# Attention output split into halves once, kept in DRAM for the MLP's second half; low halves of later weights on VectorE

## The chip, the cores and the metric

The kernel runs on one core of a Trainium2 chip. A core has TensorE (PE, matmuls, with its weight loads shown apart as PEld), VectorE (DVE), ScalarE (ACT), GpSimd (POOL) and SyncE (SP), which here only issues DMAs. Each engine takes its own instructions strictly in order and waits for others by semaphores. The metric is the device time of one execution in microseconds.

## The reference, cut to what matters

Attention with rotary embedding over 4 batches, 8 heads, 576 positions and head size 64; its output, reordered to x of 2304 tokens by 512, goes through two MLPs:

```python
x = np.ascontiguousarray(attn_out.transpose(0, 2, 1, 3)).reshape(B * S, H * D)
# first MLP: w_in 512 x 2048, w_out 2048 x 512
h = x @ w_in
g = h - np.tanh(h)
x = g @ w_out
# second MLP: w1, w2 512 x 1024, w3 1024 x 1024, w_out 1024 x 512
a = x @ w1
b = x @ w2
h = a * b @ w3
out = h @ w_out
```

The weights arrive as float64 and are read as pairs of 32-bit words.

## The kernel before, in words

**Halves.** A float32 factor is split into a high part, rounded to the type that TensorE takes (F32R), and a low part, the rest. A product is three matmuls: high by high, high by low, low by high. For weights the function `split` (L126) makes the high part on ScalarE (L127) and the low part on GpSimd (L128). For x the function `split_x` (L526) makes both on GpSimd (L528 and L529).

**Weights.** `load_raw` loads 512 KB of raw words on SP's queue into one of two buffers; `to_f32` makes float32 of them with two operations on ScalarE (L117, L119) and two on VectorE (L120, L122); `place` calls `split` into a slot. `next_conv` converts the next unit and issues the load of the one after the next. The order of the units is `half1` (`w_in` and `w_out`, first 1024 hidden units), the first part of w3 by the last `w_out` (`o2`, `w3`), `half2` (hidden units 1024 to 2047), the second part of that product, and `half3` (w1, w2). The slots of `half2` are those of `half1`, those of `half3` those of `half2`, so the conversions crowd at the turn from one to the next.

**Stages of the profiled execution.** Until about 323 us: attention. In it 16 pairs of heads run; VectorE takes row maxima (L329), ScalarE the exponentials (L336), GpSimd the normalization (L347), TensorE scores, transposes and products. From there to 809 us: the first MLP. Its tokens form five blocks: x0, x1, x2, the 256 tail tokens xt (block 4) and x3 (block 3), in this order, each with 8 steps of 128 hidden units, all of it twice, for the first and for the second half of the hidden units: `seq`, 80 steps, of which 0 to 39 are the first half. Step n is an h group (L546, 12 matmuls), `emit_g` (L559 to L569) and an x2 group (L583, 12 matmuls); h is emitted two steps ahead. `emit_g` computes h − tanh(h) on ScalarE (L559 to L562, L568) and VectorE (L563 to L566, L569) with a series for small h. The matrix w3 by the last `w_out` is folded in between (`wp_trans`, `wp_mm`) and goes to DRAM (`wp_dram`). From 809 us: the final stage, with w1, w2 and the folded matrix (`wpt`), whose input x2 is split by the same `split_x`.

**Splits of x.** The blocks are split once for each half, so twice: block p+1's first two of four parts in steps 5 and 6 of block p, the other two in step 7 (L714 to L721). The tiles `xs` share six buffers (X_BUFS) of 128 by 2 by 512; part 2 of the next block waits for a part of the current block to be free.

**Order.** The program's text gives a priority; a list scheduler of the framework places the instructions on each engine, and may hoist one out of a later stage where its inputs and buffers are ready. Conversions of `half1` that the text puts behind the attention stand within it on the engines for this reason.

## Time and profile before

| | |
|---|---|
| Median of 3 runs (lowest, highest) | 1117.77 us (1115.21, 1119.29) |
| Profiled execution, its own time | 1111.25 us |
| Its span, first to last instruction | 1109.4 us |
| TensorE busy | 1055.3 us, 95% |
| VectorE busy | 730.3 us, 66% |
| ScalarE busy | 598.9 us, 54% |
| GpSimd busy | 387.8 us, 35% |
| DMA queue q1 | 95.38 MB, 30.0% of 16 engines' span |

The shares are means over stages with different limits, so they tell little by themselves. A busy TensorE is not one at full speed: matmuls overlap, and their ends are modelled. The granted clock is 1.00 at 2.4 GHz; 0.86 in a stretch means that part of it ran at 1.2 GHz. DMA-issuing instructions and waits are not counted as busy.

### The profile page before, as it was taken

What the parts mean: (1) busy time and instruction counts of PE and PEld (TensorE: products, weight loads), DVE (VectorE), ACT (ScalarE), POOL (GpSimd) and SP (SyncE); (2) the same over time, 40 slices, a digit from 0 to 9 for tenths busy, and PEclk for the clock granted to TensorE, in tenths of its full rate; (3) what the DMA queues carried; (4) which work ended last, traced back from release to release, by engine and by line L of the source; (5) the groups of instructions that cost most, each with busy time, mean ns of one, the idle gap of its engine ahead of it and who ended that gap; (6) DMA issues with size and microseconds to landing.
All of it is one profiled execution on the core that took longest, in us unless ns stands there. A gap on an engine that the chain in (4) does not pass through costs nothing.

```text
span 1109.4 us, 15634 instructions
## 1 busy us (share of the span) xinstructions
PE 1055.3 (95%) x5598; PEld 853.6 (77%) x5598; DVE 730.3 (66%) x1300; ACT 598.9 (54%) x1262; POOL 387.8 (35%) x379
## 2 busy tenths in 40 slices
PE   5999999999998999998989999999799999999998
PEld 3777776777766888887767788898588888888887
DVE  6899988999649867669998867678952212212121
ACT  4688777777767655557767655556652111111121
POOL 5576675665461302014463220323630202001000
PEclk9899999999998999999999999999999999999999
DMA  6667675766403011023223102232740100101010
GB/s 195 171 161 173 182 178 140 186 176 147 99 20 106 10 57 58 32 64 95 77 76 113 38 10 76 87 105 86 246 133 1 38 1 1 38 1 38 1 38 20
DMA packets 64684, 96.36 MB, mean 87 GB/s; under 512 B 11616, under 2 KB 40288, under 8 KB 64608
## 3 DMA queue, kind: packets, MB, share of 16 engines
q1 hardware_dynamic: 64608, 95.38, 30.0%
q8 instruction: 44, 0.72, 0.3%
q14 instruction: 32, 0.26, 0.1%
HBM read 58.79 MB, written 11.01 MB: 63 GB/s over the span
## 4 chain that ended last, share of the span: by engine, by line
PE 68%; DVE 14%; ACT 7%; POOL 4%; DMA 4%; issue 2%; SPq 0%; DVEq 0%; ACTq 0%; POOLq 0%
PE pw L750 18%; PE x2p L583 11%; PE h L546 10%; PE o L773 9%; PE sc L325 6%; PE pv L410 4%; PE wp L630 3%; PE te L383 3%; DVE nm L329 2%; DMA raw_w<-in_moe_w 2%; DVE g_q L564 2%; ACT e L336 1%; DVE g_q L566 1%; PE pv L407 1%; DVE g_s L563 1%
## 5 line engine op out<-in xcount | busy, mean ns | idle before, releaser
L583 PE MATMUL x2p<-g,s_out 128*128 128x512 f32 (+1 forms) x960 | 223.4, 380 | 22.3 <-ACT g L568 12.8
L583 PEld LDWEIGHTS x2p<-g,s_out 128*128 128x128 f32 x960 | 172.2, 194 | 62.8 <-ACT g L568 18.3
L347 POOL TENSOR_SCALAR e<-e,r 128x576 f32<-128x576 f32 x144 | 121.8, 859 | 80.9 <-DVE r L345 35.8
L756 DVE TENSOR_TENSOR ab<-a,pw 128x512 f32<-128x512 f32 (+1 forms) x40 | 25.4, 635 | 182.9 <-PE pw L750 180.5
L336 ACT ACTIVATE e<-sc,nm 128x576 f32<-128x576 f32 x144 | 108.0, 750 | 47.2 <-DVE nm L329 31.5
L329 DVE TENSOR_REDUCE nm<-sc 128x1 f32<-128x576 f32 x144 | 106.8, 749 | 17.3 <-PE sc L325 16.5
L773 PE MATMUL o<-wpt,abs 128*128 128x512 f32 x432 | 104.5, 389 | 0.0
L325 PE MATMUL sc<-ks,qs 128*128 128x288 f32 x480 | 92.1, 321 | 3.2 <-ACT e L336 2.8
L563 DVE TENSOR_TENSOR g_s<-g_s,h 128x512 f32<-128x512 f32 (+1 forms) x80 | 50.5, 632 | 65.8 <-ACT g_m L562 65.6
L773 PEld LDWEIGHTS o<-wpt,abs 128*128 128x128 f32 x432 | 80.6, 188 | 16.4
L325 PEld LDWEIGHTS sc<-ks,qs 128*128 128x128 f32 x480 | 68.8, 190 | 26.7 <-ACT e L336 10.6
L383 PE MATMUL te<-ident,e 128*128 128x128 f32 x576 | 84.4, 278 | 5.1 <-POOL e L347 4.5
L754 ACT COPY a<-pw 128x512 f32<-128x512 f32 (+1 forms) x40 | 21.8, 544 | 117.9 <-PE pw L750 117.9
L568 ACT CAST g<-g_q 128x512 fp32r<-128x512 f32 (+1 forms) x80 | 46.1, 576 | 59.0 <-DVE g_q L566 58.6
L383 PEld LDWEIGHTS te<-ident,e 128*128 128x128 f32 x576 | 68.0, 142 | 11.7 <-POOL e L347 8.4
L559 ACT ACTIVATE g_s<-h 128x512 f32<-128x512 f32 (+1 forms) x80 | 44.1, 551 | 53.9 <-PE h L546 52.4
L569 DVE TENSOR_TENSOR g<-g_q,g 128x512 fp32r<-128x512 f32 (+1 forms) x80 | 58.1, 726 | 22.6 <-ACT g L568 21.7
L566 DVE COPY_PREDICATED g_q<-g_m,g_t 128x512 f32<-128x512 int32 (+1 forms) x80 | 69.1, 864 | 1.6
L758 ACT CAST abs<-ab 128x512 fp32r<-128x512 f32 (+1 forms) x40 | 23.0, 576 | 84.8 <-DVE ab L756 84.8
L564 DVE SCALAR_TENSOR_TENSOR g_q<-g_q,g_s 128x512 f32<-128x512 f32 (+1 forms) x80 | 62.6, 782 | 0.0
L560 ACT ACTIVATE g_q<-g_s,qb 128x512 f32<-128x512 f32 (+1 forms) x80 | 54.5, 682 | 0.2 <-DVE g L569 0.2
L562 ACT ACTIVATE g_m<-g_s,nt 128x512 f32<-128x512 f32 (+1 forms) x80 | 54.0, 676 | 0.0
(380 smaller groups left out, 2256.7 us busy)
## 6 DMA issues: line engine op xcount, KB each, us to landing
ks<-kp SPq DMA_DIRECT2D x60, 288.0 KB, 5.0
raw_w<-in_moe_w SPq DMA_DIRECT2D x32, 512.0 KB, 3.7
raw_in<-in_moe_w_in SPq DMA_DIRECT2D x16, 512.0 KB, 4.0
raw_out<-in_moe_w_out SPq DMA_DIRECT2D x16, 512.0 KB, 4.4
qs<-qp SPq DMA_DIRECT2D x60, 128.0 KB, 3.5
wp_dram<-wpe SPq DMA_DIRECT2D x24, 256.0 KB, 2.0
k<-in_k SPq DMA_DIRECT2D x16, 256.0 KB, 3.2
q<-in_q SPq DMA_DIRECT2D x16, 256.0 KB, 3.0
```

Of the source, the lines that this page charges most:

```text
L325: nc.tensor.matmul(s[:, n, 0:HS], lhs, rhs, start=t == 0, stop=t == len(terms) - 1)
L329: nc.vector.tensor_reduce(nm[:, j:j + 1], s[:, :, 0:HS], AX.XY, ALU.max, negate=True)
L336: nc.scalar.activation(d["e"][:, j, :].rearrange("p (n s) -> p n s", n=2), d["ss"][j][:, :, 0:HS], AF.Exp, bias=d["nm"][:, j:j + 1], accum ...
L347: nc.gpsimd.tensor_scalar(d["e"][:, j, :], d["e"][:, j, :], r[:, j:j + 1], 1.0, ALU.mult, ALU.mult)
L383: nc.tensor.transpose(ps[:, n * 128:(n + 1) * 128], e[:, o + n * 128:o + (n + 1) * 128], ident)
L546: nc.tensor.matmul(ps[:, 0:w], ws[:, a, kk], x[:, b_, 0:w], start=kc == 0 and t == 0, stop=kc == NK - 1 and t == 2)
L563: nc.vector.tensor_tensor(s, s, h, ALU.mult)
L564: nc.vector.scalar_tensor_tensor(qq, qq, QC, s, ALU.add, ALU.mult)
L566: nc.vector.copy_predicated(qq, mk.bitcast(I32), t)
L583: nc.tensor.matmul(x2ps[j][o][:, 0:w], ws[:, a, oo], g[:, b_, 0:w], start=c == 0 and t == 0, stop=c == HF - 1 and t == 2)
L750: nc.tensor.matmul(ps[:, 0:w], ws[:, a, kk], x[:, b_, 0:w], start=kc == 0 and t == 0, stop=kc == NK - 1 and t == 2)
L773: nc.tensor.matmul(outps[j][t], g[:, a, tt], wp[c][:, b_, :], start=c == 0 and i == 0, stop=c == NF2 - 1 and i == 2)
```

## The change

The tiles that `split_x` makes in the first half are written to DRAM (`xs_dram`, one tensor for each block) on SP's queue. In the second half `load_x` reads them back, in step 1 of the block before, instead of splitting again. Parts 2 and 3 of the blocks at places 0, 2 and 4 of the order go to the area of x3, which is then free, the others to `xs` buffers. From the end of the attention's text on, `split` makes the low part on VectorE: `lows[0]` is changed there. Counted over the program, 47 low parts (L128 before, L133 after) go from GpSimd to VectorE, and GpSimd loses the 20 splits (40 instructions) of the second half.

```diff
--- before.py
+++ after.py
@@ -78,6 +78,9 @@
     const.tile([128, 8], F32, name="half_line")
 
     wp_dram = dram.tile([DF2, 2, DM], F32, name="wp_dram")
+
+    xs_dram = [dram.tile([DM, 2, SM if j < B else B * ST], F32, name=f"xs_dram{j}")
+               for j in range(B + 1)]
 
     def slot(i, u):
         return slots.tile([128, 2, 512], F32R, tag=f"s{i}", name=f"s_{u[0]}{u[1]}")
@@ -123,9 +126,11 @@
             z, hi, -0x80000000, z, ALU.bitwise_and, ALU.bitwise_or)
         return z.bitcast(F32)
 
+    lows = [nc.gpsimd]
+
     def split(z, s):
         nc.scalar.copy(s[:, 0, :], z)
-        nc.gpsimd.tensor_tensor(s[:, 1, :], z, f32(s[:, 0, :]), ALU.subtract)
+        lows[0].tensor_tensor(s[:, 1, :], z, f32(s[:, 0, :]), ALU.subtract)
 
 
     pairs = [(b, hp) for b in range(B) for hp in range(NP)]
@@ -510,6 +515,7 @@
             pv(b, hp, c // 2)
     att.release()
     psum.release()
+    lows[0] = nc.vector
 
 
     ph2 = tc.alloc_tile_pool(name="ph2", bufs=2, side="right", reuse_waits="tile")
@@ -523,12 +529,26 @@
 
     xs = {}
 
-    def split_x(key, src, kc, w):
+    def split_x(key, src, kc, w, keep=None):
         t = ph2.tile([128, 2, SM], F32R, tag="xs", name=f"xs_{key}_{kc}", bufs=X_BUFS)
         nc.gpsimd.tensor_scalar(t[:, 0, 0:w], src[:, kc, :], 1.0, 1.0, ALU.mult, ALU.mult)
         nc.gpsimd.tensor_tensor(t[:, 1, 0:w], src[:, kc, :], f32(t[:, 0, 0:w]), ALU.subtract)
+        if keep is not None:
+            nc.sync.dma_start(keep[kc * 128:(kc + 1) * 128], f32(t[:, :, 0:w]))
         xs[key, kc] = t
 
+    def load_x(key, j, kc, w):
+
+        if order.index(j) % 2 == 0 and kc >= 2:
+            if kc == 2:
+                pair_x[0] = xpool.tile([128, 2, 2, SM], F32R, tag="x3", name=f"xl_{j}")
+            t = pair_x[0][:, kc - 2]
+        else:
+            t = ph2.tile([128, 2, SM], F32R, tag="xs", name=f"xl_{j}_{kc}", bufs=X_BUFS)
+        nc.sync.dma_start(f32(t[:, :, 0:w]), xs_dram[j][kc * 128:(kc + 1) * 128])
+        xs[key, kc] = t
+
+    pair_x = [None]
 
     order = [*range(B - 1), B, B - 1]
     seq = [(hf, j, c) for hf in range(2) for j in order for c in range(HF)]
@@ -646,7 +666,7 @@
 
     NS = len(seq)
     for kc in range(NK):
-        split_x((0, 0), x_t[0], kc, widths[0])
+        split_x((0, 0), x_t[0], kc, widths[0], xs_dram[0])
     emit_h(0)
     emit_g(0)
     emit_h(1)
@@ -711,14 +731,15 @@
             emit_h(m)
             emit_g(m)
 
-            if c2 in (HF - 3, HF - 2):
-                if m + HF - c2 < NS:
-                    hf3, j3, _ = seq[m + HF - c2]
-                    split_x((hf3, j3), x_t[j3], c2 - (HF - 3), widths[j3])
-            if c2 == HF - 1 and m + 1 < NS:
-                hf3, j3, _ = seq[m + 1]
-                for kc in (2, 3):
-                    split_x((hf3, j3), x_t[j3], kc, widths[j3])
+            p2 = order.index(j2) + hf2 * nblk
+            if c2 in (HF - 3, HF - 2, HF - 1) and p2 + 1 < nblk:
+                j3 = order[p2 + 1]
+                for kc in ((2, 3) if c2 == HF - 1 else (c2 - (HF - 3),)):
+                    split_x((0, j3), x_t[j3], kc, widths[j3], xs_dram[j3])
+            if c2 == 1 and nblk <= p2 + 1 < 2 * nblk:
+                j3 = order[p2 + 1 - nblk]
+                for kc in range(NK):
+                    load_x((1, j3), j3, kc, widths[j3])
         emit_x2(n)
         do(n)
```

In the order of instructions the names carry the step or unit, and at their ends a running number; line numbers of the changed kernel are its own, up to 20 higher.

VectorE, `emit_g` of step 44 (first MLP, second half) and the conversions among it, before:

```order
L563 TENSOR_TENSOR g_s_44_6639<-g_s_44_6639,h_44_6626 128x512
L565 TENSOR_TENSOR g_t_44_6641<-h_44_6626,g_t_44_6641 128x512
L564 SCALAR_TENSOR_TENSOR g_q_44_6640<-g_q_44_6640,g_s_44_6639 128x512
L120 SCALAR_TENSOR_TENSOR z_o27_7227<-z_o27_7227,raw_o27_7124 128x512
L566 COPY_PREDICATED g_q_44_6640<-g_m_44_6642,g_t_44_6641 128x512
L122 SCALAR_TENSOR_TENSOR z_o27_7227<-raw_o27_7124,z_o27_7227 128x512
L120 SCALAR_TENSOR_TENSOR z_w31_7276<-z_w31_7276,raw_w31_7176 128x512
L569 TENSOR_TENSOR g_44_6651<-g_q_44_6640,g_44_6651 128x512
L122 SCALAR_TENSOR_TENSOR z_w31_7276<-raw_w31_7176,z_w31_7276 128x512
```

VectorE, the same step after; L133 is the low part of a weight, L123 and L125 are the conversion (L120 and L122 before), L583 to L589 are `emit_g`:

```order
L583 TENSOR_TENSOR g_s_44_6667<-g_s_44_6667,h_44_6654 128x512
L585 TENSOR_TENSOR g_t_44_6669<-h_44_6654,g_t_44_6669 128x512
L584 SCALAR_TENSOR_TENSOR g_q_44_6668<-g_q_44_6668,g_s_44_6667 128x512
L133 TENSOR_TENSOR s_out15_6831<-z_out15_6824,s_out15_6831 128x512
L586 COPY_PREDICATED g_q_44_6668<-g_m_44_6670,g_t_44_6669 128x512
L123 SCALAR_TENSOR_TENSOR z_o24_7089<-z_o24_7089,raw_o24_6819 128x512
L125 SCALAR_TENSOR_TENSOR z_o24_7089<-raw_o24_6819,z_o24_7089 128x512
L589 TENSOR_TENSOR g_44_6679<-g_q_44_6668,g_44_6679 128x512
```

One low part, that of `s_out15`, stands between the third and the fourth operation of the chain; a unit is converted in this step as before, an earlier one than before, and only one.

SP, the loads of raw weights around the turn to the second half, before:

```order
L100 DMA raw_out12_6517<-in_moe_w_out 128x512
L94 DMA raw_in13_6611<-in_moe_w_in 128x4x128
L100 DMA raw_out13_6621<-in_moe_w_out 128x512
L94 DMA raw_in14_6671<-in_moe_w_in 128x4x128
L100 DMA raw_out14_6681<-in_moe_w_out 128x512
L94 DMA raw_in15_6734<-in_moe_w_in 128x4x128
```

SP after, where `xl_1` are the four parts of block 1:

```order
L103 DMA raw_out12_6545<-in_moe_w_out 128x512
L97 DMA raw_in13_6639<-in_moe_w_in 128x4x128
L103 DMA raw_out13_6649<-in_moe_w_out 128x512
L548 DMA xl_1_0_6515<-xs_dram1_87 128x1024
L548 DMA xl_1_1_6517<-xs_dram1_87 128x1024
L548 DMA xl_1_2_6519<-xs_dram1_87 128x1024
L548 DMA xl_1_3_6521<-xs_dram1_87 128x1024
L97 DMA raw_in14_6699<-in_moe_w_in 128x4x128
L103 DMA raw_out14_6709<-in_moe_w_out 128x512
L97 DMA raw_in15_6759<-in_moe_w_in 128x4x128
```

The four reads of block 1 stand between the loads of `raw_out13` and `raw_in14`.

ScalarE at the end of the first MLP, steps 78 and 79, with the conversions of `w13` and `w23`, before:

```order
L117 ACTIVATE z_w13_8727<-raw_w13_8594 128x512
L119 ACTIVATE raw_w13_8594<-raw_w13_8594 128x512
L117 ACTIVATE z_w23_8737<-raw_w23_8604 128x512
L559 ACTIVATE g_s_79_8534<-h_79_8521 128x512
L568 CAST g_78_8506<-g_q_78_8495 128x512
L560 ACTIVATE g_q_79_8535<-g_s_79_8534,qb_80 128x512
L561 ACTIVATE g_t_79_8536<-h_79_8521 128x512
L562 ACTIVATE g_m_79_8537<-g_s_79_8534,nt2_82 128x512
L127 CAST s_w13_8734<-z_w13_8727 128x512
L119 ACTIVATE raw_w23_8604<-raw_w23_8604 128x512
```

ScalarE at the same place after (L120, L122 and L132 are L117, L119 and L127 before; L579 to L582 and L588 are `emit_g`):

```order
L582 ACTIVATE g_m_78_8499<-g_s_78_8496,nt2_82 128x512
L132 CAST s_w22_8608<-z_w22_8601 128x512
L122 ACTIVATE raw_w13_8596<-raw_w13_8596 128x512
L579 ACTIVATE g_s_79_8536<-h_79_8523 128x512
L581 ACTIVATE g_t_79_8538<-h_79_8523 128x512
L580 ACTIVATE g_q_79_8537<-g_s_79_8536,qb_80 128x512
L588 CAST g_78_8508<-g_q_78_8497 128x512
L582 ACTIVATE g_m_79_8539<-g_s_79_8536,nt2_82 128x512
L132 CAST s_w13_8736<-z_w13_8729 128x512
L120 ACTIVATE z_w23_8739<-raw_w23_8606 128x512
L122 ACTIVATE raw_w23_8606<-raw_w23_8606 128x512
L588 CAST g_79_8548<-g_q_79_8537 128x512
```

The first operation on `raw_w23` stood ahead of `g_s_79`; it now stands behind the operations of step 79 up to `g_m_79`.

## Rows read from the trace of the kernel before

**Rows 1.** Stages, all engines: window in us, its length; busy us (instructions) of each engine; clock; DMA.

```profile
165.00:275.00 110.00, 103.80 (x750) 79.83 (x747) 103.41 (x235) 85.29 (x218) 66.58 (x72) 1.00 0.64 162
323.00:350.00 27.00, 22.82 (x92) 18.03 (x89) 22.02 (x24) 17.97 (x32) 14.63 (x12) 0.87 0.16 59
505.00:522.00 17.00, 14.13 (x83) 11.99 (x82) 15.49 (x22) 11.28 (x26) 11.08 (x9) 1.00 0.35 115
522.00:638.00 116.00, 105.80 (x437) 81.77 (x436) 103.21 (x138) 81.76 (x146) 48.00 (x35) 0.99 0.23 73
785.00:809.00 24.00, 17.07 (x61) 13.05 (x60) 21.44 (x24) 13.54 (x25) 15.49 (x12) 0.86 0.65 230
```

**Rows 2.** Waits of TensorE, 480 to 940 us: total us, times, longest.

```profile
PE x2p L583 <- ACT g L568: 8.6, 6, 3.0
...
PE x2p L583 <- DVE g L569: 7.2, 10, 1.6
...
PE h L546 <- POOL xs_(1, 0)_3_6402 L529: 2.2, 1, 2.2
```

**Rows 3.** Chain of waits, 630 to 640 us: start us, length, instructions.

```profile
632.39 2.72 PE x2p L583 x12
635.11 2.72 PE h L546 x12
```

**Rows 4.** Timeline of TensorE, 522 to 523 us: start us, length, instruction.

```profile
522.52 0.50 PE L583 MATMUL x2p<-g,s_out 128*128 128x512 f32 x1
```

**Rows 5.** Groups by line, VectorE, 522 to 638 us: count, busy us, mean ns, idle before.

```profile
L566 DVE COPY_PREDICATED g_q<-g_m,g_t 128x512 f32<-128x512 int32 x19 | 20.7, 1090 | 0.3
...
L564 DVE SCALAR_TENSOR_TENSOR g_q<-g_q,g_s 128x512 f32<-128x512 f32 x19 | 17.2, 903 | 0.0
...
L569 DVE TENSOR_TENSOR g<-g_q,g 128x512 fp32r<-128x512 f32 x19 | 14.9, 783 | 4.5 <-ACT g L568 4.1
...
L563 DVE TENSOR_TENSOR g_s<-g_s,h 128x512 f32<-128x512 f32 x19 | 13.0, 683 | 6.5 <-ACT g_m L562 6.4
...
L120 DVE SCALAR_TENSOR_TENSOR z_out<-z_out,raw_out 128x512 int32<-128x512 int32 x5 | 5.0, 1008 | 0.2 <-ACT z_out L117 0.2
```

**Rows 6.** Timeline of VectorE, 641 to 645 and 782 to 783 us, GpSimd idle.

```profile
641.99 0.68 DVE L564 SCALAR_TENSOR_TENSOR g_q<-g_q,g_s 128x512 f32<-128x512 f32 x1
642.71 0.75 DVE L566 COPY_PREDICATED g_q<-g_m,g_t 128x512 f32<-128x512 int32 x1
644.45 0.69 DVE L569 TENSOR_TENSOR g<-g_q,g 128x512 fp32r<-128x512 f32 x1 [0.99 <-ACT g L568]
...
782.40 0.69 DVE L120 SCALAR_TENSOR_TENSOR z_w<-z_w,raw_w 128x512 int32<-128x512 int32 x1
```

**Rows 7.** Timeline of VectorE, 327 to 334 us; in brackets the idle time before.

```profile
327.42 4.75 DVE L120 SCALAR_TENSOR_TENSOR z_o<-z_o,raw_o 128x512 int32<-128x512 int32 x1 [3.42 <-ACT z_o L117]
...
333.80 0.67 DVE L563 TENSOR_TENSOR g_s<-g_s,h 128x512 f32<-128x512 f32 x1
```

**Rows 8.** Groups by line, GpSimd, 522 to 638 us: count, busy us, mean ns.

```profile
L128 POOL TENSOR_TENSOR s_in<-z_in,s_in 128x512 fp32r<-128x512 f32 x6 | 10.0, 1668 | 1.4 <-ACT s_in L127 1.4
L128 POOL TENSOR_TENSOR s_out<-z_out,s_out 128x512 fp32r<-128x512 f32 x6 | 8.2, 1375 | 23.0 <-ACT s_out L127 23.0
```

**Rows 9.** Timeline of ScalarE and TensorE, 794 to 805 us; in brackets the idle time before.

```profile
794.32 0.66 ACT L117 ACTIVATE z_w<-raw_w 128x512 f32<-128x512 f32 x1 [2.81 <-DMA raw_w<-in_moe_w]
...
794.89 0.58 ACT L559 ACTIVATE g_s<-h 128x512 f32<-128x512 f32 x1
...
796.03 0.50 PE L583 MATMUL x2p<-g,s_out 128*128 128x512 f32 x1 [3.02 <-ACT g L568]
...
804.66 0.79 PE L583 MATMUL x2p<-g,s_out 128*128 128x512 f32 x1 [2.69 <-ACT g L568]
```

**Rows 10.** DMA issues by tensor: count, KB each, median us to landing.

```profile
raw_in<-in_moe_w_in SPq DMA_DIRECT2D x16, 512.0 KB, 4.0
...
wpt<-wp_dram SPq DMA_DIRECT2D x8, 512.0 KB, 7.1
```

## The prediction

> **What bounds the kernel now.** I read the windows by stage first. What can be gained in the MLP lies where TensorE is not busy throughout: its start (323 to 350), the turn from the first half of the hidden units to the second (505 to 638) and the last 24 us before the final stage (785 to 809, clock 0.86) [rows 1]. In the attention (165 to 275) TensorE and VectorE are both busy 94% of the time, so there either one may set the pace. Next, the waits of TensorE from 480 to 940 us: it waits for ScalarE's `g` (L568), VectorE's `g` (L569) and once for a split on GpSimd, L529 [rows 2]. Each is an end of the chain h, `emit_g`, x2. Third, the pace: at full speed an h group and an x2 group of 12 matmuls take 2.72 us each, so a step of the MLP takes 5.44 us. From the x2 group of step 32 of `seq`, which starts at 522.52, to that of step 49 at 632.39 lie 17 steps in 109.87 us; at full speed they need 92.5, and step 49 itself runs at full speed. So 17.4 us are lost in steps 32 to 49, which take 115.3 instead of 97.9 [rows 3, 4].
>
> The cause is VectorE. In 522 to 638 it is busy 103.2 of 116 us [rows 1], and its operations are stretched: COPY_PREDICATED (L566) takes 1090 ns on average, L564 903, L569 783, L120 of the conversion 1008 [rows 5], where the same operations take 750, 680, 690 and 690 with GpSimd idle [rows 6]. L563, which reads its second input from PSUM, is at 683 in the same window and is not stretched [rows 5]. So only operations whose inputs are all in SBUF suffer, and GpSimd is busy 48 of these 116 us [rows 1]. The worst is one L120 of 4.75 us at 327.42 [rows 7].
>
> The Trainium skill, "SBUF — State Buffer", section "SBUF: two separate sides", says that a VectorE operation with two SBUF inputs and a GpSimd operation that reads SBUF exclude each other for a whole instruction. The difference between L563 and the others agrees [rows 5]. By that rule alone one VectorE operation would lose at most one GpSimd instruction; the 4.75 us lost more than two of the 1.38 to 1.67 us splits [rows 7, 8], so I take the rows. The rule also speaks against the change, since the moved subtraction has two SBUF inputs; by it each of the five that fall into the attention may hold up L347 there by its own length, which lies inside the bound of +6 below.
>
> **The change part by part.** (a) 47 low halves (L128) go from GpSimd to VectorE: seven of the first half's weights, 8 `o2`, 16 and 16 of the later halves. On GpSimd one takes 1.38 to 1.67 us [rows 8]. VectorE's price is not in the trace; the nearest row is L569, the same subtraction with the same types: 0.69 us quiet, 0.78 mean in the crowded window [rows 5, 6]; the far end is a stretched L120, 1.01 [rows 5]. I take 0.69 where GpSimd has little left and 1.01 in the attention.
> (b) The 20 splits of x for the second half (L528, L529) disappear from GpSimd; 20 writes and 20 reads of DRAM appear on SP.
> (c) The scheduler reorders each engine.
>
> *Turn, steps 32 to 49.* What goes is the stretch: with the counts of the window, 19 × (1090−750) + 19 × (903−680) + 19 × (783−690) = 12.5 us for the g chain, and 5 × 0.32 = 1.6 for one group of L120: 14.1 [rows 5, 6]. Eleven more conversions have no row here; where they are stretched like this group they add up to 3, so some 17 in all. What comes is 20 splits × 0.69 = 13.8. From the order, VectorE's list for these 18 steps holds 18 × 5 operations of the chain (0.68+0.68+0.68+0.75+0.69 = 3.48: 62.6 us), 15 conversions of two operations (1.38: 20.7), 20 splits (13.8) and ten evictions from PSUM, three of half width, at or below L563's 0.68 (5.5): 102.6 us. TensorE needs 97.9, so VectorE is still the longer by 5. The chain also passes to ScalarE and back once a step; I allow 0.15 us a step for that, 2.7: 105.3 against 115.3, or −10.0; TensorE's one wait of 2.2 us for GpSimd's split [rows 2] is part of what goes. I take −10. Ends: nothing but full pace, −17; or the stretch stays half (+13.8 − 8.5 − the 2.2), +3. From 505 to 522 the splits of block 3 stay on GpSimd and TensorE idles 2.9 us [rows 1]; the L128 there leave: −1.5 (−3 to 0).
>
> *Last 24 us.* TensorE stands 3.02 and 2.69 us before the last two x2 groups [rows 9], and its clock is 0.86 in this stretch [rows 1]. At 794.32 ScalarE had waited 2.81 us for a raw weight, in front of the first operation of the last chain, L559 at 794.89 [rows 9]. In the new order this conversion (`z_w23`) stands behind that chain's ScalarE operations, its load ahead of the `wpt` loads, and the splits of the final stage's first block run earlier, because block 3's second half uses only two of the six `xs` buffers. Against that come 4 splits on VectorE, 2.8 us. Of the 24 us, whose 17.1 of busy time include the slow clock's [rows 1], I take 5 off: most of the two waits (0 to −8; 8 with the clock back).
>
> *Start, 323 to 350.* GpSimd loses 6 low halves but now splits block 1 immediately; VectorE gets 4 of them and two conversions ahead of the first L563, eight operations: 5.5 us quiet, 8 at 1.01, against the 6.4 us from the long L120 to the L563 at 333.80 now [rows 7]. I take −1 (−4 to +3).
>
> *Attention.* Five splits on a full VectorE: 5 × 1.01 = 5; GpSimd gives up 5 × 1.38 = 6.9 us that stretched others, and TensorE waits for it too: I take +2 (−2 to +6).
>
> *SP and the loads.* The writes wait for splits that GpSimd makes as early as before, and the reads are issued in step 1 of the block ahead, some 38 us before use, so TensorE's h does not wait. What they may delay is queued behind them: at the turn `raw_in14` stands behind four reads of block 1 that wait for the last h of half one. A load of a raw weight takes 4.0 us, eight 512 KB loads in short succession 7.1 [rows 10], so it lands some 4 us later after a hold of up to 5. Its conversion now stands ahead of `g_s_41` on ScalarE, before it stood ahead of `g_s_39`: two steps, 10.9 us, cover it. Price 0 (0 to +9; 9 if that cover fails, since ScalarE then holds the next chain). After 809 TensorE stays full: a step of three groups of 2.72 us holds two conversions and two splits, 4.1 us of VectorE.
>
> Sum: −10 −1.5 −5 −1 +2 = −15.5 on the profiled 1111.25 us: 1095.75. The median of the runs is 6.52 us above the profiled run; I add that: 1102.
>
> **The rivals.** *The loads give it back.* `raw_out11` behind the reads of block 0 and `raw_in14` behind those of block 1 each stop ScalarE for 4 to 5 us: −15.5 + 9 = −6.5, 1111. For it: ScalarE runs in order and already waits for raw loads [rows 9]; against: the cover above.
> *VectorE becomes the wall.* The splits stand between L564 and L566, in the chain itself. If the stretch is not GpSimd's doing, nothing is relieved and VectorE gets longer: +13.8 at the turn, +2.8 at the end, +5 in the attention: 1139. It decides for slower when less than 13.8 of the 17 us of stretch goes. L563 against the others speaks against it [rows 5].
> *Everything clears.* VectorE falls within TensorE's 5.44 us in every step: −17 −3 −7 −2 +1 = −28: 1090. Against: steps with two splits or evictions hold over 6 us.
> *The change does nothing*: the stretch goes and the added work takes all of it, 17 for 17: 1117. For it: 13.8 and 17 are near.
>
> **How the numbers follow.** Forecast 0.58, loads 0.12, wall 0.06, all clear 0.14, nothing 0.10. What a measurement can tell from no change is about 0.5%, 5.6 us. The forecast lies 16 us below the median, its own range 1093 to 1110, and reaches past 1112 with a tenth. Faster: 0.54 + 0.14 + 0.09 (most of the loads' case) + 0.02 = 0.79; same 0.13; slower 0.08. The range takes in all clear and most of the loads' case: 1089 to 1115.
>
> **What would show it.** L564, L566 and L569 at about 0.68 to 0.75 between 522 and 638; 18 steps there in about 105 us; VectorE's L128 row at about 0.7; no wait of TensorE for L529; waits before the last two x2 groups of 2 us or less in sum. I am wrong if those operations stay stretched, if ScalarE waits long for `raw_in14` or `raw_out11`, or if the attention ends more than 6 us later than its 323.

## The result, and the profile after

| | before | changed |
|---|---|---|
| median of the runs (lowest to highest), us | 1117.08 (1115.21 to 1119.29), 4 runs | 1085.84 (1084.23 to 1091.75), 4 runs |
| profiled execution: its time, its span, us | 1111.25, 1109.4 | 1086.10, 1083.9 |
| ratio to before | | 0.9729, 95% interval 0.9688 to 0.977 |

The changed kernel is 31.2 us faster by the medians and 25.6 us by the spans of the two profiled executions. The forecast was 1102 in a range of 1089 to 1115: the direction came true, the time did not; the result lies 3 us below the range.

Where the 25.6 us come from is read by stages that both kernels have. A stage ends here with a named operation: the start of the attention's row maximum 24 (counted from 0), the start of its last one, the end of VectorE's low half of `g` of steps 4, 30, 56 and 72, the end of the first low half of the final stage, and the end of the span. Lengths in us, worked out from the two traces (a part of the −1.5 forecast for 505 to 522 us lies behind g 30 and so in the turn):

| stage | before | changed | difference | forecast |
|---|---|---|---|---|
| start, to maximum 24 | 66.4 | 66.8 | +0.4 | 0 |
| attention, to the last maximum | 246.5 | 242.5 | −4.0 | +2 |
| start of the MLP, to g 4 | 47.2 | 45.8 | −1.4 | −1 |
| g 4 to g 30 | 154.0 | 153.8 | −0.2 | −1.5 |
| turn, g 30 to g 56 | 153.2 | 136.9 | −16.3 | −10 |
| g 56 to g 72 | 91.9 | 91.6 | −0.3 | 0 |
| last steps, to the final stage | 59.2 | 54.2 | −5.0 | −5 |
| final stage | 291.1 | 292.2 | +1.1 | 0 |

The windows of the changed kernel that answer to [rows 1] show the same, columns as there. The first is the same stretch; the others lie some 5 to 25 us earlier than their partners, as the changed kernel is ahead there.

```profile
165.00:275.00 110.00, 105.97 (x759) 81.66 (x758) 103.76 (x241) 86.33 (x221) 64.69 (x69) 1.00 0.67 169
318.00:345.00 27.00, 22.49 (x99) 17.54 (x99) 21.09 (x27) 16.79 (x30) 9.41 (x9) 0.94 0.41 155
500.00:517.00 17.00, 15.64 (x95) 13.70 (x95) 15.33 (x30) 12.32 (x28) 4.91 (x4) 1.00 0.79 274
517.00:620.00 103.00, 102.54 (x451) 84.10 (x450) 96.14 (x156) 84.44 (x150) 0.00 (x0) 1.00 0.38 127
760.00:784.00 24.00, 19.34 (x78) 13.80 (x77) 22.72 (x35) 15.57 (x28) 4.57 (x4) 1.00 0.68 246
```

The fourth row is the result in one line: at the turn TensorE is busy 102.5 of 103 us, GpSimd does nothing, and VectorE does 156 operations in 96.1 us, where it needed 103.2 us for 138 before. From the x2 group of step 32, at 517.35, to that of step 49, at 611.00, lie 93.65 us; with step 49 at 5.44 the 18 steps that the forecast counted take 99.1 us, where it had 105.3 and full speed is 97.9. The waits of TensorE from 460 to 915 us answer to [rows 2]; the wait for GpSimd's split is gone.

```profile
PE x2p L603 <- ACT g L588: 3.3, 4, 1.5
PE x2p L603 <- DVE g L589: 3.0, 5, 1.3
PE x2p L603 <- DVE x L613: 0.3, 1, 0.3
```

VectorE's groups from 517 to 617 us answer to [rows 5]: L586 is the L566 of before, L589 its L569, L584 its L564, L583 its L563, L123 its L120. L133 is the moved subtraction.

```profile
L586 DVE COPY_PREDICATED g_q<-g_m,g_t 128x512 f32<-128x512 int32 x19 | 14.4, 757 | 0.0
L589 DVE TENSOR_TENSOR g<-g_q,g 128x512 fp32r<-128x512 f32 x19 | 13.1, 688 | 2.8 <-ACT g L588 2.7
L583 DVE TENSOR_TENSOR g_s<-g_s,h 128x512 f32<-128x512 f32 x19 | 13.0, 684 | 2.7 <-ACT g_m L582 2.6
...
L584 DVE SCALAR_TENSOR_TENSOR g_q<-g_q,g_s 128x512 f32<-128x512 f32 x19 | 13.0, 682 | 0.0
L133 DVE TENSOR_TENSOR s_in<-z_in,s_in 128x512 fp32r<-128x512 f32 x6 | 4.1, 686 | 0.0
...
L123 DVE SCALAR_TENSOR_TENSOR z_out<-z_out,raw_out 128x512 int32<-128x512 int32 x5 | 3.4, 685 | 0.0
```

All the stretch is gone, and the moved subtraction takes 0.69 us, as forecast. What the forecast did not use stands in the starts, not in the durations. First VectorE's timeline in the changed kernel, then in the kernel before at a place in its turn where GpSimd does not disturb it:

```profile
575.53 0.69 DVE L589 TENSOR_TENSOR g<-g_q,g 128x512 fp32r<-128x512 f32 x1
576.13 0.68 DVE L583 TENSOR_TENSOR g_s<-g_s,h 128x512 f32<-128x512 f32 x1
576.73 0.68 DVE L585 TENSOR_TENSOR g_t<-h,g_t 128x512 f32<-128x512 f32 x1
577.33 0.68 DVE L584 SCALAR_TENSOR_TENSOR g_q<-g_q,g_s 128x512 f32<-128x512 f32 x1
577.93 0.68 DVE L133 TENSOR_TENSOR s_out<-z_out,s_out 128x512 fp32r<-128x512 f32 x1
578.53 0.75 DVE L586 COPY_PREDICATED g_q<-g_m,g_t 128x512 f32<-128x512 int32 x1
```

```profile
578.91 0.67 DVE L563 TENSOR_TENSOR g_s<-g_s,h 128x512 f32<-128x512 f32 x1
579.51 0.68 DVE L565 TENSOR_TENSOR g_t<-h,g_t 128x512 f32<-128x512 f32 x1
580.11 0.67 DVE L564 SCALAR_TENSOR_TENSOR g_q<-g_q,g_s 128x512 f32<-128x512 f32 x1
580.71 0.68 DVE L122 SCALAR_TENSOR_TENSOR z_out<-raw_out,z_out 128x512 int32<-128x512 int32 x1
```

An operation lasts 0.68 us, but the next starts 0.60 us after it: a full list advances by the pitch. Only where an operation reads what the one just before it wrote do 0.71 to 0.72 us pass, as between the first two of [rows 6]. The subtraction at 577.93 stands in such a gap: with it L586 starts 1.20 us after L584, without it 0.72, so it costs 0.48 us.

TensorE's last x2 groups before the final stage answer to [rows 9], in brackets the idle time before them. First a row of the kernel before that stands between the two of [rows 9], then the changed kernel:

```profile
797.75 4.21 PE L583 MATMUL x2p<-g,s_out 128*128 128x512 f32 x11 [1.22 <-DVE g L569]
```

```profile
775.18 0.73 PE L603 MATMUL x2p<-g,s_out 128*128 128x512 f32 x2 [1.47 <-ACT g L588]
776.43 2.56 PE L603 MATMUL x2p<-g,s_out 128*128 128x512 f32 x10 [0.52 <-DVE g L589]
780.11 1.20 PE L603 MATMUL x2p<-g,s_out 128*128 128x512 f32 x4 [1.13 <-ACT g L588]
```

In the last two groups 3.1 us of waiting are left of 6.9 (3.02, 1.22 and 2.69), more than the 2 that were said to show the step right; the granted clock stays at 1.00 where it was 0.86, and ten matmuls take 2.56 us where eleven took 4.21. At the MLP's start VectorE's timeline answers to [rows 7]: the 4.75 us operation is gone, the moved subtractions are stretched beside the splits of x, and the first L583 comes at 331.45.

```profile
320.81 1.71 DVE L133 TENSOR_TENSOR s_out<-z_out,s_out 128x512 fp32r<-128x512 f32 x1 [0.23 <-ACT s_out L132]
322.45 1.10 DVE L133 TENSOR_TENSOR s_in<-z_in,s_in 128x512 fp32r<-128x512 f32 x1
323.46 1.09 DVE L133 TENSOR_TENSOR o<-z_o,o 128x512 fp32r<-128x512 f32 x1
...
331.45 0.69 DVE L583 TENSOR_TENSOR g_s<-g_s,h 128x512 f32<-128x512 f32 x1 [1.51 <-ACT g_m L582]
```

### The profile page after: what moved, and what is told of

Same layout as the page of the kernel before. It is cut to its first block, busy times and chain, and to the rows that moved or that the text cites. A ratio compares the mean times of both kernels' runs of the same rounds, so it can differ in the third digit from the quotient of the medians.

```text
span 1083.9 us, 15658 instructions
## 1 busy us (share of the span) xinstructions
PE 1043.6 (96%) x5598; PEld 847.6 (78%) x5598; DVE 718.6 (66%) x1344; ACT 599.1 (55%) x1265; POOL 281.3 (26%) x292
## 4 chain that ended last, share of the span: by engine, by line
PE 69%; DVE 15%; ACT 7%; DMA 4%; issue 3%; POOL 1%; DVEq 0%; ACTq 0%; SPq 0%; POOLq 0%
PE pw L771 18%; PE x2p L603 11%; PE h L566 10%; PE o L794 9%; PE sc L330 6%; PE pv L415 5%; PE wp L650 4%; PE te L388 3%; ACT e L341 2%; DVE nm L334 2%; DVE g_q L584 1%; DVE g_q L586 1%; PE pv L412 1%; DVE g_s L583 1%; DMA raw_in<-in_moe_w_in 1%
## 5 line engine op out<-in xcount | busy, mean ns | idle before, releaser
L603 PE MATMUL x2p<-g,s_out 128*128 128x512 f32 (+1 forms) x960 | 215.7, 372 | 11.3 <-ACT g L588 7.9
L603 PEld LDWEIGHTS x2p<-g,s_out 128*128 128x128 f32 x960 | 168.8, 190 | 46.9 <-ACT g L588 9.8
L352 POOL TENSOR_SCALAR e<-e,r 128x576 f32<-128x576 f32 x144 | 124.9, 879 | 81.2 <-DVE r L350 43.0
L566 PE MATMUL h<-xl,s_in 128*128 128x512 f32 (+1 forms) x480 | 105.8, 369 | 0.0
L566 PEld LDWEIGHTS h<-xl,s_in 128*128 128x128 f32 x480 | 84.0, 188 | 15.2
L583 DVE TENSOR_TENSOR g_s<-g_s,h 128x512 f32<-128x512 f32 (+1 forms) x80 | 50.5, 631 | 62.4 <-ACT g_m L582 62.2
L588 ACT CAST g<-g_q 128x512 fp32r<-128x512 f32 (+1 forms) x80 | 46.1, 576 | 52.8 <-DVE g_q L586 52.5
L579 ACT ACTIVATE g_s<-h 128x512 f32<-128x512 f32 (+1 forms) x80 | 44.0, 550 | 52.4 <-PE h L566 52.3
L589 DVE TENSOR_TENSOR g<-g_q,g 128x512 fp32r<-128x512 f32 (+1 forms) x80 | 55.5, 693 | 22.8 <-ACT g L588 22.2
L662 POOL TENSOR_TENSOR wpe<-wpe 128x512 fp32r<-128x512 f32 x8 | 11.9, 1485 | 216.0 <-ACT wpe L661 216.0
L586 DVE COPY_PREDICATED g_q<-g_m,g_t 128x512 f32<-128x512 int32 (+1 forms) x80 | 57.1, 714 | 1.1
```

The source lines that it names most:

```text
L352: nc.gpsimd.tensor_scalar(d["e"][:, j, :], d["e"][:, j, :], r[:, j:j + 1], 1.0, ALU.mult, ALU.mult)
L566: nc.tensor.matmul(ps[:, 0:w], ws[:, a, kk], x[:, b_, 0:w], start=kc == 0 and t == 0, stop=kc == NK - 1 and t == 2)
L583: nc.vector.tensor_tensor(s, s, h, ALU.mult)
L586: nc.vector.copy_predicated(qq, mk.bitcast(I32), t)
L589: nc.vector.tensor_tensor(g[:, 1, 0:w], qq, f32(g[:, 0, 0:w]), ALU.subtract)
L603: nc.tensor.matmul(x2ps[j][o][:, 0:w], ws[:, a, oo], g[:, b_, 0:w], start=c == 0 and t == 0, stop=c == HF - 1 and t == 2)
```

## The experiments

The table gives the stages as above, in us, for each profiled run, and "rest", the time from maximum 24 to the end. The start is kept apart since it differs between executions of one kernel: 70.3 in the second profile of the changed kernel (e13) against 66.8. Those two profiles also differ by up to 1.2 us in a stage and 3.1 in the rest; smaller differences say nothing.

| run | median (range) | start | attention | to g 4 | to g 30 | turn | last steps | rest |
|---|---|---|---|---|---|---|---|---|
| before | 1117.1 | 66.4 | 246.5 | 47.2 | 154.0 | 153.2 | 59.2 | 1043.0 |
| changed | 1085.8 | 66.8 | 242.5 | 45.8 | 153.8 | 136.9 | 54.2 | 1017.0 |
| e13 changed again | 1085.3 (1081.2–1091.1) | 70.3 | 241.7 | 46.0 | 152.6 | 136.4 | 53.3 | 1013.9 |
| e1 low halves only | 1100.0 (1096.7–1104.1) | 70.6 | 241.8 | 47.1 | 154.4 | 145.2 | 59.4 | 1030.7 |
| e2 x only | 1100.1 (1096.3–1103.4) | 66.8 | 246.4 | 44.8 | 151.6 | 147.1 | 53.9 | 1028.1 |
| e3 all on VectorE | 1088.1 (1083.0–1090.8) | 74.0 | 242.2 | 46.9 | 152.0 | 136.3 | 53.3 | 1015.0 |
| e4 first half on GpSimd | 1085.0 (1081.6–1090.9) | 65.5 | 245.0 | 43.6 | 153.5 | 136.2 | 53.4 | 1015.6 |
| e5 low halves twice | 1094.6 (1088.7–1098.4) | 66.1 | 246.7 | 47.8 | 151.5 | 136.5 | 54.6 | 1020.8 |
| e6 idle reads, early | 1115.2 (1107.2–1118.8) | 73.1 | 241.8 | 50.4 | 175.1 | 136.6 | 54.5 | 1042.3 |
| e7 idle memsets, early | 1089.1 (1084.7–1094.2) | 66.1 | 241.7 | 45.8 | 154.7 | 136.3 | 54.4 | 1016.8 |
| e8 late conversions | 1087.2 (1086.6–1088.9) | 70.4 | 241.8 | 46.2 | 153.0 | 138.2 | 52.3 | 1014.4 |
| e9 idle reads on GpSimd | 1099.0 (1096.9–1101.6) | 70.5 | 241.8 | 45.7 | 153.0 | 145.8 | 54.2 | 1024.8 |
| e10 idle memsets | 1091.9 (1084.5–1092.3) | 73.3 | 243.1 | 46.5 | 153.2 | 136.4 | 54.2 | 1017.2 |
| e14 before, early matmuls | 1104.3 (1103.5–1105.5) | 61.9 | 244.7 | 45.4 | 153.7 | 153.4 | 60.0 | 1040.6 |
| e11 changed, early matmuls | 1082.3 (1081.0–1085.0) | 61.8 | 246.0 | 46.5 | 151.7 | 136.2 | 54.0 | 1018.2 |
| e12 three edits | 1083.7 (1080.9–1090.9) | 63.2 | 245.9 | 45.8 | 150.6 | 137.7 | 52.5 | 1015.4 |

**The two halves of the change (e1, e2).** e1 keeps the moved low halves and splits x again on GpSimd, without the writes to DRAM; e2 keeps the stored x and leaves `lows` on GpSimd.

```
e1:  if c2 in (HF - 3, HF - 2, HF - 1) and p2 + 1 < 2 * nblk:
         j3 = order[(p2 + 1) % nblk]
         ...  split_x(((p2 + 1) // nblk, j3), x_t[j3], kc, widths[j3])
e2: -    lows[0] = nc.vector
    +    lows[0] = nc.gpsimd
```

> Only the low halves of the weights move to VectorE; the second half's x is split again on GpSimd as before. Theory P (VectorE issues independent operations every 0.60 to 0.62 us, although one lasts 0.68): its list of some 148 operations in steps 32 to 49 takes 91 us plus the stretch that 21 us of GpSimd's splits of x still cause (17 x 21/48 = 7), 98 against TensorE's 97.9, so nearly the whole turn is won: 14 to 17 there, 3 more in the attention, 2 to 4 at the end; 1091 to 1098. Theory D (the sum on record: a VectorE operation costs its duration): 102.6 + 7 + 2.7 = 112 at the turn, so 3 won there, total 1100 to 1106. Rival S (TensorE's waits for GpSimd's splits of x were the real loss at the turn): hardly any gain there, 1105 to 1112.

> Only the split x goes to DRAM and comes back; the low halves stay on GpSimd everywhere. P: VectorE's list loses 20 operations (128 at 0.62: 79 us) and keeps a stretch of 17 x 27/48 = 10: 89 against 97.9, full pace at the turn, 15 to 17 won, nothing in the attention, 2 to 3 at the end: 1095 to 1100. D: 88.8 + 10 + 2.7 = 101.5 at the turn, 13 won, 1 to 3 at the end: 1099 to 1103. S: as P.

Ratios 0.986 [0.9818, 0.9903] and 0.9858 [0.9817, 0.99]. At the turn e1 wins 8.0 us and e2 6.1 of the 16.3: less than theory P said for either, while D missed in both directions (3 and 13). In the rest −12.3 and −14.9 add up to −27.2 against −26.0 for both together. So the change is two halves of about equal worth in time; the attention's 4 us come with the low halves, and the 5 us of the last steps with the stored x.

Rival S, that TensorE's waits for GpSimd's splits of x were the loss, is out by e1: the splits are back there, and all that TensorE waits for from 514 to 659 us, e1's turn, is `g` of VectorE and ScalarE:

```profile
PE x2p L603 <- DVE g L589: 5.8, 4, 2.1
PE x2p L603 <- ACT g L588: 0.9, 1, 0.9
```

In the kernel before, 2.2 of the 11.8 us of such waits in its turn (514 to 667 us) were for a split.

Why half a relief wins less than in proportion, e1 shows. GpSimd's splits come in bursts; VectorE's timeline in one of them:

```profile
552.27 1.17 DVE L586 COPY_PREDICATED g_q<-g_m,g_t 128x512 f32<-128x512 int32 x1
553.33 1.78 DVE L123 SCALAR_TENSOR_TENSOR z_in<-z_in,raw_in 128x512 int32<-128x512 int32 x1
555.15 1.67 DVE L125 SCALAR_TENSOR_TENSOR z_in<-raw_in,z_in 128x512 int32<-128x512 int32 x1
556.74 1.09 DVE L589 TENSOR_TENSOR g<-g_q,g 128x512 fp32r<-128x512 f32 x1
557.75 0.68 DVE L583 TENSOR_TENSOR g_s<-g_s,h 128x512 f32<-128x512 f32 x1
```

and all engines in three stretches around the next one (columns as in [rows 1]), then TensorE's x2 group in the second of them:

```profile
590.00:600.00 10.00, 10.00 (x45) 8.27 (x45) 8.91 (x13) 7.74 (x14) 5.76 (x6) 1.00 0.37 107
600.00:610.00 10.00, 6.96 (x20) 4.99 (x19) 9.90 (x14) 5.92 (x11) 3.79 (x3) 0.71 0.15 53
610.00:620.00 10.00, 10.00 (x43) 8.25 (x42) 9.37 (x16) 6.71 (x13) 0.00 (x0) 0.95 0.16 53
```

```profile
605.08 5.06 PE L603 MATMUL x2p<-g,s_out 128*128 128x512 f32 x11 [2.11 <-DVE g L589]
```

Four operations in a row take 1.1 to 1.8 us. Over 100 us that is little, but at once it is more than the chain is ahead of TensorE. TensorE then stops, and after the stop its granted clock is 0.71 in the second row: part of that stretch runs at the lower of its two levels, and the eleven matmuls behind the stop take 5.06 us. So a stop of 2.1 us costs more than itself.

**How much room VectorE has (e5).**

```
         lows[0].tensor_tensor(s[:, 1, :], z, f32(s[:, 0, :]), ALU.subtract)
+        if lows[0] is nc.vector:
+            nc.vector.tensor_tensor(s[:, 1, :], z, f32(s[:, 0, :]), ALU.subtract)
```

> The changed kernel with each low half that VectorE makes from the MLP on written twice, by the same subtraction: 46 more VectorE operations, 20 of them in the 18 steps of the turn. In the changed kernel VectorE is busy 94.1 of the 100 us from 510 to 610 us and TensorE 99.5. Theory W: the 5.9 us of VectorE's idle time are the hand-overs to ScalarE and no slack, so VectorE and TensorE are both at their wall there, and each added operation costs its pitch: 20 x 0.6 = 12 at the turn, 2 to 3 more at the start and the end; 1099 to 1103. Theory L: these 5.9 us are slack and take half of the added work: 6 at the turn, 1092 to 1096. Theory D (the sum on record, operations at their duration, VectorE the longer already): 13.8 at the turn, 3 elsewhere, 1102 to 1105.

Ratio 0.9839 [0.9784, 0.9894], but not one of the 8.8 us of loss lies at the turn: 136.5 against 136.9. All three theories missed there; the median falls into L's range for another reason. VectorE takes the added operations in full, and TensorE does not notice (503 to 633 us):

```profile
503.00:633.00 130.00, 128.98 (x592) 106.51 (x591) 126.10 (x210) 102.04 (x188) 4.54 (x4) 1.00 0.38 131
```

210 operations in 126.1 us are 0.60 each; VectorE is busy 97% of the time and TensorE 99%. So VectorE's idle time was slack, and hand-overs to ScalarE cost nothing while VectorE has other operations to put between them. In the profiled run, the fastest of the four at 1088.7 us, the loss lies in the attention (+4.2) and the MLP's start (+2.0); where the slower runs lose the rest of the 8.8 is not shown.

**Is it the stretch, or the waits for the splits? (e6, e7, e9, e10).** e6 and e7 put idle work on GpSimd.

```
e6: +  nc.gpsimd.tensor_scalar(t, x, 1.0, 1.0, ALU.mult, ALU.mult)    (x: half a chunk of x_t)
    +  nc.gpsimd.tensor_tensor(t, x, t, ALU.subtract)
e7: +  nc.gpsimd.memset(t, 0.0)
    +  nc.gpsimd.memset(t, 1.0)
```

> The changed kernel, with as much reading and writing of SBUF put back on GpSimd as the 20 splits of x of the second half made (a copy and a subtraction on each chunk of x, in halves of 256 columns, into a spare tile that nobody reads); the split x still comes from DRAM. Theory R (GpSimd's operations stretch VectorE's, and that is what made x's splits dear): the turn gets 6 to 9 us longer, as the run with x split on GpSimd was, and the whole 8 to 13: 1094 to 1099. Rival T (TensorE's and the buffers' waits for the splits made them dear): no more than 2 us, 1085 to 1088.

> As the run before, but GpSimd only writes the spare tile (memsets of the same size) and reads nothing. Theory R1 (any access of GpSimd to SBUF holds VectorE up): in proportion to GpSimd's added busy time, at 7 us of stretch to 20 us of it; with some 0.3 us for a memset, 80 of them, 24 us: 1092 to 1096. Theory R2 (it is operations of GpSimd that read SBUF): within 2 us of 1086.

Neither tests the turn: the scheduler moved the idle work to 333 to 392 us (e6) and 326 to 352 us (e7). e6 came to 1115.2 (ratio 1.0017 [0.9984, 1.0049]) because TensorE stood 18.4 us for the splits of block 1, which stood behind it on GpSimd; e7 to 1089.1 (ratio 0.981 [0.9749, 0.9871]). In e9 and e10 the idle work reads the tiles that come back from DRAM, which keeps it at the turn.

```
             load_x((1, j3), j3, kc, widths[j3])
+            x = f32(xs[(1, j3), kc][:, 0, o:o + 256])        (o = 0 and 256)
e9:  +       nc.gpsimd.tensor_scalar(t, x, 1.0, 1.0, ALU.mult, ALU.mult)
     +       nc.gpsimd.tensor_tensor(t, x, t, ALU.subtract)
e10: +       nc.gpsimd.tensor_scalar(t[:, 0:1], x[:, 0:1], 1.0, 1.0, ALU.mult, ALU.mult)
     +       for _ in range(4): nc.gpsimd.memset(t, 0.0)
```

> The two runs with idle GpSimd work had it at 326 to 392 us, not at the turn. Here the same idle work (a copy and a subtraction on each chunk, in halves of 256 columns, into a spare tile) reads the tiles of x as they come back from DRAM, so it runs when a block of the second half is loaded; nothing waits for it. Theory B (in a burst of GpSimd's operations VectorE runs at half its pace, falls more than its lead of two steps behind, and TensorE waits): COPY_PREDICATED and the subtractions beside a burst at 1.1 to 1.8 us, and the time from the low half of g of step 30 to that of step 56 longer than in the changed kernel by 3 to 8 us. Theory A (VectorE's spare time takes the stretch, as it took 20 more operations): operations as long as that, but 0 to 2 us. Theory T (the waits for the splits of x were the loss, not the stretch): no stretch and 0 us.

> As the run before, with four memsets of the spare tile for each half chunk in place of the copy and the subtraction (one column is read once, so that they come at the same place). If only operations of GpSimd that read SBUF hold VectorE up, VectorE's operations stay at 0.68 to 0.76 us and the time within 2 us of the changed kernel's; if any access does, it goes as the run before.

All engines and two of VectorE's groups from 515 to 625 us, first with the reads (e9), then with the memsets (e10):

```profile
515.00:625.00 110.00, 105.34 (x459) 84.17 (x458) 104.39 (x155) 83.33 (x150) 39.12 (x48) 1.00 0.36 128
...
L586 DVE COPY_PREDICATED g_q<-g_m,g_t 128x512 f32<-128x512 int32 x19 | 16.1, 847 | 0.0
L589 DVE TENSOR_TENSOR g<-g_q,g 128x512 fp32r<-128x512 f32 x19 | 14.7, 773 | 2.0 <-ACT g L588 1.9
```

```profile
515.00:625.00 110.00, 109.80 (x494) 90.60 (x493) 103.01 (x172) 90.76 (x163) 39.35 (x120) 1.00 0.41 145
...
L586 DVE COPY_PREDICATED g_q<-g_m,g_t 128x512 f32<-128x512 int32 x20 | 15.2, 758 | 0.0
L589 DVE TENSOR_TENSOR g<-g_q,g 128x512 fp32r<-128x512 f32 x20 | 13.8, 689 | 2.9 <-ACT g L588 2.6
```

GpSimd is busy 39 us in both. With reads VectorE's operations are stretched, beside the bursts to 1.1 to 1.3 us (theory B had 1.1 to 1.8), and the turn takes 145.8 us, 8.9 more (B had 3 to 8), although nothing waits for GpSimd's work: TensorE's waits in it, 4.5 us in sum, are for VectorE's L589 and L613. With memsets these waits are 0.2 us, the turn takes 136.4, like the changed kernel, and VectorE's operations keep their length; the median of 1091.9 goes with a start of 73.3, and the rest is 1017.2 for 1017.0. The ratios are 0.9861 [0.9819, 0.9902] and 0.9774 [0.9723, 0.9826]. So operations of GpSimd that read SBUF are the cause of the stretch and of TensorE's waits, and waits for the splits need not be. The rule that the prediction drew from "SBUF — State Buffer" in the Trainium skill ("SBUF: two separate sides") names just these: against a VectorE operation with two SBUF inputs only a GpSimd operation that reads SBUF counts. Here the trace agrees.

**The attention (e3, e4).** e3 puts every low half on VectorE, also the nine that the attention's schedule had left on GpSimd; e4 leaves the first half's weights on GpSimd and switches at the first `conv_o2`.

```
e3: -    lows = [nc.gpsimd]
    +    lows = [nc.vector]
e4: -    lows[0] = nc.vector           (behind psum.release())
         def conv_o2(i, r):
    +        lows[0] = nc.vector
```

> The changed kernel with all low halves on VectorE, those of the attention's nine remaining too. If relief of GpSimd is what made the attention 3.5 to 4 us shorter with five moved (R), nine more give 3 to 8 us: 1078 to 1083. If an added VectorE operation in the attention costs its time (C, as the sum on record had it), 9 x 0.6 to 1.0 = 5 to 9 us longer, less at most as much as GpSimd gave up: 1086 to 1094. If the gain in the attention came from the new order alone (O), no telling, within 3 us of 1086.

> The changed kernel, but the seven low halves of the first half's weights, five of which the scheduler had put into the attention, go back to GpSimd. R: the attention takes 3.5 to 4 us longer again: 1089 to 1091. C: it gets shorter or stays: 1083 to 1086. O: within 3 us of 1086, and the attention's end is not tied to the count of moved halves.

Ratios 0.9747 [0.9707, 0.9787] and 0.9738 [0.9689, 0.9788]: neither differs from the changed kernel, so R's times for both runs missed. In the stages, with the five halves back on GpSimd the attention takes 245.0, so 2.5 of the 4.0 us go; with all on VectorE 242.2, so the others bring nothing; with the five made twice (e5) 246.7. That fits R for the five, though 2.5 is less than its 3.5 to 4, and e4 gets it back at the MLP's start (43.6); for the others the relief and the cost come out even. With the early matmuls (e11 against e14), which also changed the order of the attention, the five cost 1.3 us. So the attention's term depends on the order around it, between −4.0 and +1.3; why is not settled.

**The last steps (e8).** Conversions of the final stage's weights are kept out of the last 24 us by writing four of them into a buffer that block 3 holds until its last h.

```
+    def late_z(i):
+        if not z3:
+            z3.append(xpool.tile([128, EARLY, 512], I32, tag="x3", name="z_late"))
+        return z3[0][:, i - EARLY, :]
...
-                at(p, conv_z, None)
+                at(p, conv_z, (lambda i=i: late_z(i)) if hf and i < 2 * EARLY else None)
```

> The changed kernel, where the conversions of the four weights after the first four of the final stage write a buffer that comes free only when the last h group has read x, so that they leave the last 24 us of the MLP, in which VectorE is busy 22.7 of 24 us and TensorE waits 6.4. If VectorE's and ScalarE's conversions in there are what stops TensorE (theory V): 4 to 6 us shorter, 1080 to 1082, with TensorE's waits before the last x2 groups at 2 us or less. If it is the chain's own length (theory C: h, ScalarE, VectorE, ScalarE, VectorE, x2 with nothing else to do for TensorE): within 1 us of 1086. If the final stage then waits for its weights: longer by up to 5.

The median is 1087.2, no gain by the runs (ratio 0.978 [0.9735, 0.9824]). The last steps take 52.3 us, 1.0 and 1.9 less than in the two profiles of the changed kernel. TensorE's waits for `g` before the final stage are 2.2 us in sum, where the changed kernel has 4.6 and 3.9 in its two profiles (not 6.4, as the expectation says). So the conversions made about half of the waiting, and V got at most half of the time that it expected; that the other half is the chain's own is argued.

**The start (e11, e13, e14).** Four matmuls of zeros before TensorE's first operand, in the changed kernel (e11) and in the kernel before (e14); e13 is the changed kernel unchanged.

```
+    warm = x_t[0][:, 0, :]
+    nc.vector.memset(warm, 0.0)
+    wps_ = psum.tile([128, 512], F32, tag="t", name="warm", bufs=4)
+    for _ in range(4):
+        nc.tensor.matmul(wps_, warm[:, 0:128], warm, start=True, stop=True)
```

> The changed kernel with four matmuls of 128 x 512 zeros at the start of TensorE's list, before its first operand has come (8 us), whose result nobody reads. In the profiled runs so far a matmul of 288 columns takes about twice as long until 17, 30 or 40 us from the start, and the 24th row maximum comes at 65.5 to 74.0 us; the runs of one kernel lie in groups some 6 us apart. Theory K (the groups, and the 6.5 us between the median of the kernel before and its profiled run, are when TensorE gets its full pace at the start): all runs of this kernel end early, 1080 to 1086, with a spread under 4 us, and the 24th maximum comes at or before 66. If the extra work only delays the start: 1087 to 1092 with the groups still there.

> The changed kernel once more, for the share of its runs in which TensorE gets its pace early. Theory K: its runs lie in groups, near 1085 and near 1091, so its median is anywhere between, and the 31.2 us between the medians hold up to 6 us of that; from the 24th maximum on the two kernels differ by 26.0. Otherwise the runs lie within 3 us of 1086.

> The kernel before with the four early matmuls, for a comparison without these groups. Theory K: spread under 4 us, 1104 to 1109, and the changed kernel with the same matmuls (1082.3) shorter by 23 to 26 us. If the matmuls were good for something else in the changed kernel: 1110 to 1117, in groups.

TensorE's first matmuls of 288 columns, 15 to 30 us, in the kernel before, in e1 and in e11:

```profile
L325 PE MATMUL sc<-k_first,q_first 64*128 64x288 f32 x31 | 10.2, 454 | 0.0
```

```profile
L330 PE MATMUL sc<-k_first,q_first 64*128 64x288 f32 x20 | 10.3, 724 | 0.0
```

```profile
L330 PE MATMUL sc<-k_first,q_first 64*128 64x288 f32 x32 | 9.7, 429 | 0.0
```

The starts of the profiled runs without early matmuls fall into three groups: 65.5 to 66.8, 70.3 to 70.6 and 73.1 to 74.0 us. With them it is 61.8 to 63.2. The kernel before then runs in 1103.5 to 1105.5, the changed one in 1081.0 to 1085.0; the 46 runs of the kernel before on record lie between 1107.0 and 1119.3. The spread of e14 is 2.0 us (ratio 0.9915 [0.9885, 0.9945]), that of e11 4.0, and e13's six runs lie from 1081.2 to 1086.0 and at 1091.1 (ratio 0.9746 [0.971, 0.9781]). Theory K holds for the kernel before. For the changed kernel it holds in part: e12, which has the same matmuls and an early start (63.2), still has runs at 1086.3 and 1090.9, a spread of 10.0 us, so the start is not all that differs between runs. The two kernels with early matmuls are 22.0 us apart, not 23 to 26; from row maximum 24 on the profiled runs of the two kernels differ by 22.4 (e14 and e11) to 29.1 us (before and e13). So the change is worth some 22 to 29 us. That the unprofiled runs fall into the same groups, and that the rest of the 31.2 between the first medians is the draw of the start, is argued from their times, not shown.

**All together (e12).** Early matmuls, late conversions, and the last two chunks of block 3 split by ScalarE and VectorE.

```
+        if key == (0, B - 1) and kc >= 2:
+            nc.scalar.copy(t[:, 0, 0:w], src[:, kc, :])
+            nc.vector.tensor_tensor(t[:, 1, 0:w], src[:, kc, :], f32(t[:, 0, 0:w]), ALU.subtract)
```

> The changed kernel with three edits that the runs point to: the four early matmuls; the late buffer for four weights of the final stage (from the 24th row maximum on, that run was 2.7 us shorter than the changed kernel); and the splits of the last two chunks of block 3 in the first half made by ScalarE and VectorE, so that GpSimd's burst at 505 to 515 us, beside which TensorE loses some 3 us, is half as long. From 1082.3: 2.7 for the second, 1 to 2 for the third: 1077 to 1080. If VectorE's and ScalarE's added operations there cost what the burst did, 1079 to 1081; if the final stage waits for its weights, above 1082.

The profiled run has the shortest span of all, 1078.6 us, but the median is 1083.7 (ratio 0.9742 [0.9703, 0.9782]), above e11's 1082.3 and above the 1077 to 1081 expected, though the final stage got no longer (291.2 us). So the three edits are not shown to be better; e11 has the lowest median and beats the kernel before by 2.9% (ratio 0.9714 [0.9682, 0.9747]), while its interval overlaps that of the changed kernel.

## Why the prediction was wrong

**The cause was right.** The stretch, its source and its place came out as told: L564, L566 and L569 fell to 0.68, 0.76 and 0.69 us, the moved subtraction takes 0.69, no wait for a split is left, and e9 against e10 shows the source. It also held that the loads cost nothing: ScalarE waits for `raw_in` and `raw_out` at most 1.4 us at a time from 500 to 600 us, though the reads of x land 5.9 us after issue in the median. The MLP's start came out at −1.4 for −1, and g 4 to g 30 at −0.2 for −1.5. The last steps came out at −5.0 as forecast, but by another sum: the forecast took most of the two waits, 5.7 us; TensorE's idle time in these 24 us fell from 6.9 to 4.7, and most of the rest goes with the clock, 0.86 before and 1.00 after, which stood only in its bound. That hit is in part luck.

**The step that failed is VectorE's list at the turn.** The prediction counted 102.6 us for its operations, durations added up, found that 5 us longer than TensorE's 97.9, and put 2.7 us of hand-overs on top: 105.3. Its some 148 operations advance by the pitch: at the 0.616 us that 96.14 us for 156 operations give, 91 us, below TensorE's 97.9. And the hand-overs cost nothing (e5). The turn therefore went nearly to TensorE's full pace: 16.3 us instead of 10. This is the rival "Everything clears", whose −17 there is what came; its "steps with two splits or evictions hold over 6 us" was the same mistake, since nine operations at 0.60 us are 5.4, and a step of TensorE is 5.44. The trace before held the pitch in its turn, as shown above. By the pitch the list of before would have fitted too: 128 operations at 0.616 us are 79, with the 17 of stretch that it counted 96, and VectorE stood idle in 12.8 of the 116 us [rows 1]. So the kernel before did not lose its 17 us because VectorE's list was longer in sum. Its losses come in bursts, as in e1 and e9, with a lower clock behind a stop, and a sum over the whole turn holds neither; the share of each was not measured. Its own worst 10 us (columns as in [rows 1]): GpSimd is busy 9.5, nine operations of VectorE take 9.2, and TensorE is busy 7.8 at a clock of 0.83.

```profile
560.00:570.00 10.00, 7.81 (x26) 5.94 (x26) 9.18 (x9) 5.14 (x11) 9.46 (x6) 0.83 0.25 62
```

**Attention.** The five moved subtractions cost what was forecast, 4.5 us in sum for 5 (0.80, 0.68, 1.70, 0.68 and 0.68, the 1.70 stretched by GpSimd). But the stage got 4.0 us shorter instead of 2 longer. VectorE's operations sum to 252.5 us there as before (252.7), with three operations more, as two others left the stage: most of what the five add, others lost in stretch. So the cost stands (five more in e5: 4.2 us longer), and the term that was set too small is the relief of GpSimd. Why TensorE then gains 4 us in one order and loses 1.3 in another is open.

**The 6.52 us** added for the distance of the profiled run from the median were a step too many: the profiled run of the changed kernel lies at its median. That they were the draw of the start in the kernel before is argued, as said under e14. Of the 16.2 us between forecast and result these are 6.8, the turn 6.3, the attention 6.0; what is left, 2.9 the other way, are the small terms.

**The other rivals.** VectorE did not become the wall: e5 gives it 8% more operations there (210 in 130 us; the changed kernel has 194 in 500 to 630) without loss. The loads gave nothing back, and the gain was not eaten by the added work.

## What to carry to other kernels

Add up an in-order engine's list by the distance between starts in a full stretch, not by durations; here 155 operations of 107.5 us in sum fit into 96.1 us of busy time, and that decided whether VectorE or TensorE is the wall. Before moving work onto a busy engine, look at what shares SBUF with it: operations of GpSimd that read SBUF cost VectorE more than the moved work did, and in bursts, which a lead of two steps does not cover. A sum over a stretch doesn't show bursts: look at the waits one by one. Compare kernels by stages that begin behind the start, and don't add the distance between a profiled run and the median to a forecast before its cause is known.
